# Two weight subtractions on GpSimd instead of VectorE, with a new order of the instructions

## The chip, the core and the metric

The kernel runs on one core of a Trainium2 chip. The metric is the device time in microseconds from the start to the end of one execution. The core has five engines that work side by side, each on its own list of instructions in a fixed order: PE (TensorE, the matmuls; PEld is its loading of weights), DVE (VectorE), ACT (ScalarE), POOL (GpSimd), and SP, which here only issues DMAs. They wait for each other through semaphores.

## The reference

Attention within chunks of 64 tokens is followed by a feed-forward layer with a quadratic relu. All inputs are float32.

```python
# q, k, v: 8 batches x 8 heads x 576 tokens x 64
scores = q_c @ k_c.T / sqrt(64)           # within each chunk of 64 tokens
attn = exp(scores - max); attn = attn / (sum + 1e-9)
x = (attn @ v_c)                          # as 4608 tokens x 512
h = x @ w_in                              # w_in 512 x 2048
g = where(h >= 1, h, where(h <= -1, 0, (h + 1) ** 2 / 4))
out = g @ w_out                           # w_out 2048 x 512
```

The two weights come as 64-bit floats; the kernel reads them as pairs of 32-bit words.

## The kernel before, in words

**Tiles.** The 4608 tokens are nine tiles of 512. `w_in` and `w_out` are cut into 16 blocks each (wi0 to wi15, wo0 to wo15). A product in full precision is three matmuls: each operand is kept as a high part (rounded to the matmul's format) and a low part (what the rounding left), and high x high, high x low and low x high are summed in PSUM.

**Preparing weights** (`prepare`, L433 to 479). A block lands as words; ACT scales the upper words (L444), DVE shifts (L447), ACT scales the lower words (L450), DVE adds (L455), ACT rounds to the high part (L470), and DVE subtracts to get the low part (L474). So a block costs three instructions on ACT and three on DVE.

**Stages.** First comes the attention of tile 0, in four groups of two heads: PE turns q and k (L569), ACT copies (L594), PE makes scores (L617), DVE and ACT do the softmax (L696 to L709, L702), POOL multiplies by the reciprocal sum (L714), PE turns the result back (L569), ACT copies (L725), PE multiplies by v (L638), and ACT and DVE split the result into high and low part, xh and xl (L779, L780). While PE has nothing else to do there it runs matmuls on the identity that nobody reads (L1535, called fillers here). Then the first three tiles go through the layer directly (`ffn_in` L831, the curve at L838, L841 and L842, the split at L851 and L852, `ffn_out` L866), while the blocks of weights are still being prepared and the attention of later tiles is done in between. The last six tiles go in pairs by a scheme that needs seven products of mixed blocks instead of eight (L1103). For it, sums of the weights' blocks are formed (`mix_weights`, L936 to L960), written to DRAM by POOL's DMAs (L922) and later streamed back by POOL's DMAs (L1011) into a ring of seven places; and sums of the inputs are formed for each pair (`mix_x`, L1074 to L1083). In the paired stage L1112, L1118, L1144, L1147, L1148 are the sums and the curve, and L1202 and L1203 split the middle result into high and low part.

**What sets the order.** A planner (`Plan`) takes all steps with an assumed cost for each, their inputs and outputs, plays them through in its own model of the engines and of the DMA queues, and lets each engine take the ready step with the earliest deadline. It does so twice to get deadlines and then writes the instructions in the order that results. Steps that carry an `after` (the mixing of the weights) get a deadline earlier by `EARLY`. Fillers are written wherever the model finds PE without work between two given points. So a change of one cost, or of one entry of a table, can move instructions on every engine; and how many fillers the program has is fixed when it is written.

Of the kernel before, what the change touches and what calls it, by code (L numbers as in the profile page):

```python
# [62 lines left out]
class Plan:  # L63
# [9 lines left out]
    ROUNDS = 2  # L73
    EARLY = 5.0
    PACKET = {128: 0.0128, 256: 0.0188, 512: 0.031, 1024: 0.05, 2048: 0.086, 4096: 0.22}
# [186 lines left out]
def kernel(  # L262
# [15 lines left out]
    nc = tc.nc  # L278
# [14 lines left out]
    NF = DFF // P  # L293
# [5 lines left out]
    ROWED = (0, 1)  # L299
    EARLY = 2  # L300

# [9 lines left out]
    OWN, RING5, EARLIER, LATER, SPARE = range(5)  # L311
    SCHEDULE = (
        (17, OWN), (18, EARLIER), (18, OWN), (21, EARLIER), (22, RING5), (24, RING5), (25, EARLIER), (27, OWN), (27, RING5), (33, RING5), (37, LATER), (38, OWN), (42, RING5), (43, OWN), (45, OWN), (46, OWN),
    )
# [66 lines left out]
    for w, j, names in (  # L381
# [5 lines left out]
        both = place("first", w, j, [P, 2, T], F32)  # L387
# [13 lines left out]
    plan = Plan()  # L401
# [31 lines left out]
    def prepare(w, j):  # L433
# [38 lines left out]
        def low():  # L472
            hi, lo = (weight[w, j][:, n, :] for n in range(2))
            nc.vector.tensor_tensor(  # L474
                out=placed(lo), in0=natural(yf), in1=placed(hi.bitcast(F32)), op=ALU.subtract
            )

        plan.add("act", 0.52, high, (ykey,), both)
        plan.add("dve", 0.6, low, (ykey, both[0]), (both[1],))


# [502 lines left out]
    LOADS = list(range((NTILE - MIXED) // 2 * STEPS // 2))  # L984
    for load, sooner in ((5, 1), (10, 1), (14, 1), (56, 2), (70, 1), (112, 2), (126, 1), (154, 1),):
        was = LOADS.index(load)
        LOADS.insert(was - sooner, LOADS.pop(was))
    TAKEN = {11: 1, 12: 1, 14: 1, 16: 1, 20: 1, 61: 1, 62: 1, 76: 1, 117: 1, 118: 1, 132: 1, 160: 1}
    held, SLOT, OUSTED = [(tag, -1) for tag in RING], {}, {}
# [405 lines left out]
    FIRST_SCORES, BURSTS = 4, (4, 8, 11, 15)  # L1395
    PAIRS = {0: (BURSTS[-1],), 1: (5, 12), 2: (0, 4, 9, 12)}
    HELD_BURSTS, RECALL_BURSTS, HELD_MIX_X = (0, 2, 4, 6), (6, 11), 1
    QUAD_BURSTS, OUT_BURST, MIX_X = (0, 4, 6), 1, 0
    MIX_AT = []
    for n, own in SCHEDULE:  # L1400
        m = len(MIX_AT)
        what = ("wi", m) if m < NF // 2 else ("wo", (4, 1, 5, 2, 0, 3, 6, 7)[m - NF // 2])
        MIX_AT.append((n, own, what))
# [99 lines left out]
    def mix_next(t):  # L1503
        plan.behind = 0
        mix_x(t)
        plan.behind = 0
# [68 lines left out]
```

## Time and profile before

| | |
|---|---|
| time, median of 3 runs | 797.57 us (797.56 to 798.97) |
| the profiled execution | 798.37 us, of which the span from first to last instruction 796.6 us |
| granted TensorE clock, mean | 0.999 of full speed |
| busy: PE, DVE, ACT, POOL | 99%, 86%, 63%, 22% of the span |
| chain that ended last | PE 81%, DVE 10%, DMA 3%, ACT 3%, SP's queue 2% |

The busy shares are averages over very different stages. PE counts as busy while it runs fillers too, so its 99% does not say that 99% of the span is useful work. Overlapping matmuls make each record longer than the distance between two starts; the distance is what counts.

### The profile page before, as it was taken

How to read it: one execution, taken by the hardware profiler on the slowest of the kernel's cores; microseconds unless marked ns; L12 is line 12 of the kernel's file. 1: busy time of each engine (PE TensorE's matmuls, PEld its weight loads, DVE VectorE, ACT ScalarE, POOL GpSimd, SP SyncE). 2: the span in 40 equal slices, each digit the busy share in tenths (PEclk: the TensorE clock that was granted, in tenths of full speed). 3: DMA queues.
4: the chain of work that ended last, by engine and by line, in shares of the span. 5: the costliest groups of instructions: out<-in, count | busy, mean ns of one | idle time of the engine just before them, and what ended most of it. 6: DMA issues, size and time to landing. Idle time of an engine off the chain costs nothing.

```text
span 796.6 us, 15281 instructions
## 1 busy us (share of the span) xinstructions
PE 787.3 (99%) x5660; PEld 650.2 (82%) x5660; DVE 682.8 (86%) x1089; ACT 501.7 (63%) x870; POOL 179.0 (22%) x294
## 2 busy tenths in 40 slices
PE   9999999999999999999999999999999999999997
PEld 8788888888888888888887888788878888888886
DVE  4989998798867899999969999999599986765896
ACT  5999874454555466776468646864687456636840
POOL 1100000756132233223221211111111121211211
PEclk9999999999999999999999999999999999999999
DMA  9996855979598777989899868998765697566664
GB/s 203 282 296 166 212 103 105 328 239 305 152 275 235 188 214 225 247 286 261 244 275 255 219 182 224 294 274 235 211 205 175 188 278 231 186 192 190 193 190 106
DMA packets 250571, 176.67 MB, mean 222 GB/s; under 512 B 208129, under 2 KB 216321, under 8 KB 250497
## 3 DMA queue, kind: packets, MB, share of 16 engines
q0 software_dynamic: 33344, 117.98, 46.5%
q1 hardware_dynamic: 212896, 56.66, 31.9%
q10 hardware_dynamic: 4256, 1.05, 0.7%
q8 instruction: 45, 0.74, 0.4%
q14 instruction: 30, 0.24, 0.1%
HBM read 133.17 MB, written 38.80 MB: 216 GB/s over the span
## 4 chain that ended last, share of the span: by engine, by line
PE 81%; DVE 10%; DMA 3%; ACT 3%; SPq 2%; issue 1%; DVEq 0%
PE ps_o L1103 34%; PE ps_o L866 17%; PE ps_h L831 15%; PE ps_h L1103 11%; PE ps_a L617 2%; DVE big_wo L1112 1%; DVE big_wo L1148 1%; PE ps_h L638 1%; DVE gl L1203 1%; DVE big_wo L1203 1%; DMA words_wi<-in_moe_w_in_dram 1%; DVE big_wo L1122 1%; DMA q_sb_both<-in_q_dram 1%; SPq L493 1%; DMA aT_both<-qT_both 1%
## 5 line engine op out<-in xcount | busy, mean ns | idle before, releaser
L1011 POOL DMA_DIRECT2D big_wi<-mixed x144 | 77.0, 535 | 328.2 <-PE ps_o L1103 175.6
L831 PE MATMUL ps_h<-xh,parts_wi 128*128 128x512 f32 x376 | 125.4, 393 | 0.7 <-DVE r L842 0.7
L866 PE MATMUL ps_o<-parts_wo,gh 128*128 128x512 f32 x384 | 119.8, 393 | 0.0
L1103 PE MATMUL ps_o<-big_wo,big_wi 128*128 128x512 f32 x396 | 96.5, 389 | 0.0
L1103 PE MATMUL ps_o<-gh,big_wi 128*128 128x512 f32 x264 | 88.5, 390 | 0.0
L1103 PEld LDWEIGHTS ps_o<-big_wo,big_wi 128*128 128x128 f32 x396 | 74.3, 188 | 15.5
L866 PEld LDWEIGHTS ps_o<-parts_wo,gh 128*128 128x128 f32 x384 | 71.1, 188 | 15.4 <-ACT tmp L888 0.4
L831 PEld LDWEIGHTS ps_h<-xh,parts_wi 128*128 128x128 f32 x376 | 70.6, 188 | 15.8 <-DVE r L842 1.1
L1103 PE MATMUL ps_h<-big_wi,big_wi 128*128 128x512 f32 x312 | 75.9, 390 | 0.0
L866 PE MATMUL ps_o<-parts_wo,gl 128*128 128x512 f32 x192 | 74.9, 390 | 0.0
L831 PE MATMUL ps_h<-xl,parts_wi 128*128 128x512 f32 x188 | 73.2, 389 | 0.0
L1103 PE MATMUL ps_o<-big_wi,big_wi 128*128 128x512 f32 x282 | 71.0, 392 | 1.2 <-ACT tmp L1118 1.2
L1202 ACT CAST big_wo<-big_wo 128x512 fp32r<-128x512 f32 x76 | 47.1, 621 | 35.0 <-PE ps_o L1103 20.2
L1103 PEld LDWEIGHTS ps_h<-big_wi,big_wi 128*128 128x128 f32 x312 | 58.4, 188 | 12.2
L1202 ACT CAST gh<-big_wo 128x512 fp32r<-128x512 f32 x76 | 47.1, 620 | 27.4 <-PE ps_o L1103 23.2
L1103 PEld LDWEIGHTS ps_o<-big_wi,big_wi 128*128 128x128 f32 x282 | 52.3, 188 | 14.2 <-ACT tmp L1118 2.7
L1147 ACT ACTIVATE big_wo<-big_wo 128x512 f32<-128x512 f32 x96 | 60.0, 632 | 1.6
L1103 PEld LDWEIGHTS ps_o<-gh,big_wi 128*128 128x128 f32 x264 | 49.6, 188 | 10.7 <-ACT big_xl L795 0.2
L1112 DVE TENSOR_TENSOR big_wo<-ps_o,big_wo 128x512 f32<-128x512 f32 x84 | 56.0, 680 | 1.9 <-PE ps_o L1103 1.8
L1203 DVE TENSOR_TENSOR gl<-big_wo,gh 128x512 fp32r<-128x512 f32 x76 | 51.8, 681 | 6.2 <-ACT gh L1202 6.2
L1203 DVE TENSOR_TENSOR big_wo<-big_wo,big_wo 128x512 fp32r<-128x512 f32 x76 | 51.7, 683 | 4.4 <-ACT big_wo L1202 4.3
L1103 PE MATMUL ps_o<-gl,big_wi 128*128 128x512 f32 x132 | 51.4, 389 | 0.0
(283 smaller groups left out, 1647.6 us busy)
## 6 DMA issues: line engine op xcount, KB each, us to landing
big_wi<-mixed POOLq DMA_DIRECT2D x144, 512.0 KB, 4.7
big_wo<-mixed POOLq DMA_DIRECT2D x24, 512.0 KB, 4.8
words_wi<-in_moe_w_in_dram SPq DMA_DIRECT2D x16, 512.0 KB, 6.4
words_wo<-in_moe_w_out_dram SPq DMA_DIRECT2D x16, 512.0 KB, 6.6
v_sb<-in_v_dram SPq DMA_DIRECT2D x52, 128.0 KB, 4.6
q_sb_both<-in_q_dram SPq DMA_DIRECT2D x104, 64.0 KB, 4.2
k_sb_both<-in_k_dram SPq DMA_DIRECT2D x104, 64.0 KB, 3.8
mixed<-parts_wi POOLq DMA_DIRECT2D x24, 256.0 KB, 4.6
```

Of the source, the lines that this page charges most:

```text
L493: queue.dma_start(out=dst[j * C:(j + 1) * C], in_=heads_rows(src, t, 2 * g + j).rearrange("c p d -> p c d"),)
L617: nc.tensor.matmul(out=scores[i * C:(i + 1) * C, half, n * C:(n + 1) * C], lhsT=qT[rows, at], rhs=kT[rows, at], start=True, stop=True,)
L638: nc.tensor.matmul(out=values[half][h * C:(h + 1) * C, n * C:(n + 1) * C], lhsT=v_sb[rows, of:of + C], rhs=rhs, start=True, stop=True,)
L831: nc.tensor.matmul(out=ps, lhsT=weight["wi", j][:, half, kc * P:(kc + 1) * P], rhs=x(), start=(kc == 0 and i == 0), stop=(kc == KC - 1 and ...
L866: nc.tensor.matmul(out=acc, lhsT=x[:, cols], rhs=weight["wo", j][:, half, :], start=(j == 0 and i == 0), stop=(j == NF - 1 and i == 2),)
L1011: nc.gpsimd.dma_start(out=place_of(tag).bitcast(F32), in_=mixed[n][:, rows, :])
L1103: nc.tensor.matmul(out=bank, lhsT=parts[part], rhs=rhs, start=fresh and begin and k == 0, stop=end and k == 2, skip_group_check=not fresh,)
L1112: plan.add("dve", cost, lambda: nc.vector.tensor_tensor(out=o(), in0=b, in1=x(), op=ALU.add), (bkey, xkey), (okey,), after=after)
L1122: plan.add("dve", 0.6, lambda: nc.vector.tensor_tensor(out=o(), in0=x(), in1=y(), op=ALU.subtract), (xkey, ykey), (okey,))
L1147: plan.add("act", 0.52, lambda: nc.scalar.square(out=r(), in_=r()), (), (rkey,))
L1202: plan.add("act", 0.52, lambda: nc.scalar.copy(out=h(), in_=x()), (key,), (hkey,))
L1203: plan.add("dve", 0.6, lambda: nc.vector.tensor_tensor(out=l(), in0=x(), in1=h().bitcast(F32), op=ALU.subtract), (key, hkey), (lkey,))
```

## The change

The low part (L474) of wi0 and of wo0 is computed by POOL instead of DVE, with 1.1 us as its assumed cost. `EARLY` goes from 5 to 50 us. The tables that place the mixing of the weights, the loads of the ring, the attention of a later tile and the mixing of the inputs (`SCHEDULE`, `LOADS`, `TAKEN`, `PAIRS`, `MIX_X`, the sequence of `wo`) get other entries, and `mix_x` starts with another rank. The number of DVE's instructions falls by two, POOL's rises by two; the other engines do the same work.

```diff
-    EARLY = 5.0
+    EARLY = 50.0
...
     OWN, RING5, EARLIER, LATER, SPARE = range(5)
     SCHEDULE = (
-        (17, OWN), (18, EARLIER), (18, OWN), (21, EARLIER), (22, RING5), (24, RING5), (25, EARLIER), (27, OWN), (27, RING5), (33, RING5), (37, LATER), (38, OWN), (42, RING5), (43, OWN), (45, OWN), (46, OWN),
+        (18, OWN), (19, EARLIER), (20, RING5), (21, EARLIER), (22, EARLIER), (22, OWN), (24, RING5), (27, RING5), (34, RING5), (37, LATER), (37, LATER), (37, OWN), (43, OWN), (43, OWN), (44, OWN), (47, OWN),
     )
...
             hi, lo = (weight[w, j][:, n, :] for n in range(2))
-            nc.vector.tensor_tensor(
+            (nc.gpsimd if j < 1 else nc.vector).tensor_tensor(
                 out=placed(lo), in0=natural(yf), in1=placed(hi.bitcast(F32)), op=ALU.subtract
             )
 
         plan.add("act", 0.52, high, (ykey,), both)
-        plan.add("dve", 0.6, low, (ykey, both[0]), (both[1],))
+        plan.add(*(("pool", 1.1) if j < 1 else ("dve", 0.6)), low, (ykey, both[0]), (both[1],))
...
-    for load, sooner in ((5, 1), (10, 1), (14, 1), (56, 2), (70, 1), (112, 2), (126, 1), (154, 1),):
+    for load, sooner in ((5, 1), (10, 1), (14, 1), (56, 4), (57, 4), (58, 3), (70, 1), (112, 3), (113, 3), (126, 1), (154, 1),):
...
-    TAKEN = {11: 1, 12: 1, 14: 1, 16: 1, 20: 1, 61: 1, 62: 1, 76: 1, 117: 1, 118: 1, 132: 1, 160: 1}
+    TAKEN = {11: 1, 12: 1, 14: 1, 16: 1, 20: 1, 22: 1, 62: 1, 76: 1, 115: 1, 132: 1, 160: 1}
...
-    PAIRS = {0: (BURSTS[-1],), 1: (5, 12), 2: (0, 4, 9, 12)}
+    PAIRS = {0: (BURSTS[-1],), 1: (4, 12), 2: (0, 4, 9, 12)}
...
-    QUAD_BURSTS, OUT_BURST, MIX_X = (0, 4, 6), 1, 0
+    QUAD_BURSTS, OUT_BURST, MIX_X = (0, 4, 6), 1, 3
...
-        what = ("wi", m) if m < NF // 2 else ("wo", (4, 1, 5, 2, 0, 3, 6, 7)[m - NF // 2])
+        what = ("wi", m) if m < NF // 2 else ("wo", (2, 1, 5, 6, 0, 4, 3, 7)[m - NF // 2])
...
     def mix_next(t):
-        plan.behind = 0
+        plan.behind = 60
         mix_x(t)
```


On SP, whose list is only DMA issues at this place, from the load of k of group 2 on. The places first_wi15 and first_wi14 take q and k of groups 2 and 3, the places v_sb0, v_sb1 and first_wo14 the values of groups 0 to 2. Before:

```order
L493 DMA first_wi14_97<-in_k_dram 64x8x64 x2
L493 DMA first_wi15_95<-in_q_dram 64x8x64 x2
L493 DMA first_wi14_97<-in_k_dram 64x8x64 x2
L420 DMA words_wi0_175<-in_moe_w_in_dram 128x4x256
L543 DMA v_sb0_70<-in_v_dram 128x4x64 x2
L543 DMA v_sb1_71<-in_v_dram 128x4x64 x2
L420 DMA words_wi1_225<-in_moe_w_in_dram 128x4x256
L543 DMA first_wo14_98<-in_v_dram 128x4x64 x2
L420 DMA words_wi2_259<-in_moe_w_in_dram 128x4x256
```

Now:

```order
L493 DMA first_wi14_97<-in_k_dram 64x8x64 x2
L420 DMA words_wi0_135<-in_moe_w_in_dram 128x4x256
L493 DMA first_wi15_95<-in_q_dram 64x8x64 x2
L493 DMA first_wi14_97<-in_k_dram 64x8x64 x2
L543 DMA v_sb0_70<-in_v_dram 128x4x64 x2
L420 DMA words_wi1_209<-in_moe_w_in_dram 128x4x256
L543 DMA v_sb1_71<-in_v_dram 128x4x64 x2
L543 DMA first_wo14_98<-in_v_dram 128x4x64 x2
L420 DMA words_wi2_269<-in_moe_w_in_dram 128x4x256
```

The load of wi0 stands in front of q and k of group 3, and the load of wi1 in front of the values of group 1. The load of wi2 has the same loads in front of it as before.

On ACT, ten rows before the curve of the first block is done (L838, L841). r0 is the middle result of wi0, ps_h0 its bank, xh1 from ps_o23 the high part of group 3. Before:

```order
L470 CAST parts_wi3_464<-tmp1_88 128x512
L779 CAST xh1_0_0_421<-ps_o23_89 128x2x4x64
L450 ACTIVATE words_wo0_324<-words_wo0_324 128x512
L444 ACTIVATE tmp_both_86<-words_wo1_327 128x512
L450 ACTIVATE words_wo1_327<-words_wo1_327 128x512
L470 CAST parts_wo0_489<-tmp0_87 128x4x4x32
L444 ACTIVATE tmp_both_86<-words_wi4_342 128x512
L838 ACTIVATE r0_80<-ps_h0_93 128x512
L838 ACTIVATE r1_81<-ps_h1_94 128x512
L841 ACTIVATE r0_80<-r0_80 128x512
```

Now, from the high part of group 3 on:

```order
L779 CAST xh1_0_0_411<-ps_o23_89 128x2x4x64
L444 ACTIVATE tmp0_87<-words_wo0_331 128x512
L470 CAST parts_wi3_465<-tmp1_88 128x512
L450 ACTIVATE words_wo0_331<-words_wo0_331 128x512
L444 ACTIVATE tmp_both_86<-words_wo1_341 128x512
L450 ACTIVATE words_wo1_341<-words_wo1_341 128x512
L838 ACTIVATE r0_80<-ps_h0_93 128x512
L470 CAST parts_wo0_493<-tmp0_87 128x4x4x32
L841 ACTIVATE r0_80<-r0_80 128x512
```

The high part of wo0 (L470 on parts_wo0) and the first step of wi4 (L444 on words_wi4) stood in front of the curve of r0 (L838) and now stand behind it. Further up on ACT, around the first step of wi2, before:

```order
L725 COPY first_wi13_99<-ps_o1_92 128x512
L779 CAST xh0_0_0_331<-ps_o23_89 128x2x4x64
L444 ACTIVATE tmp_both_86<-words_wi2_259 128x512
L450 ACTIVATE words_wi2_259<-words_wi2_259 128x512
L470 CAST parts_wi1_413<-tmp_both_86 128x512
L779 CAST xh1_0_0_421<-ps_a_90 128x2x4x64
```

Now:

```order
L725 COPY first_wi13_99<-ps_o1_92 128x512
L470 CAST parts_wi1_380<-tmp_both_86 128x512
L779 CAST xh0_0_0_320<-ps_o23_89 128x2x4x64
L444 ACTIVATE tmp_both_86<-words_wi2_269 128x512
L779 CAST xh1_0_0_411<-ps_a_90 128x2x4x64
L450 ACTIVATE words_wi2_269<-words_wi2_269 128x512
```

The high part of wi1 (L470 on parts_wi1) stood behind the first step of wi2 and now stands in front of it.

On PE, twelve rows from the turning back of the softmax of group 1 (kT_both) on; first_wo14 and first_wo15 hold the softmax of groups 2 and 3, and the one row on parts_wi0 and xl0 stands in the first product of the layer. Before:

```order
L569 MATMUL ps_o1_92<-ident_65,kT_both_76 128x128 x4
L638 MATMUL ps_a_90<-aT_both_77,v_sb0_70 64x64 x16
L1535 MATMUL ps_h0_93<-ident_65 128x128 x7
L569 MATMUL ps_o1_92<-ident_65,first_wo14_98 128x128 x4
L1535 MATMUL ps_h0_93<-ident_65 128x128
L638 MATMUL ps_o23_89<-aT_both_77,v_sb1_71 64x64 x16
L831 MATMUL ps_h0_93<-xh0_0_0_331,parts_wi0_306 128x512
L831 MATMUL ps_h0_93<-xl0_0_0_352,parts_wi0_306 128x512
L831 MATMUL ps_h0_93<-xh0_0_0_331,parts_wi0_306 128x512
L638 MATMUL ps_a_90<-first_wi13_99,first_wo14_98 64x64 x16
L1535 MATMUL ps_o0_91<-ident_65 128x128 x4
L569 MATMUL ps_o1_92<-ident_65,first_wo15_96 128x128 x4
```

Now:

```order
L569 MATMUL ps_o1_92<-ident_65,kT_both_76 128x128 x4
L1535 MATMUL ps_h0_93<-ident_65 128x128 x2
L831 MATMUL ps_h0_93<-xh0_0_0_320,parts_wi0_297 128x512
L831 MATMUL ps_h0_93<-xl0_0_0_328,parts_wi0_297 128x512
L831 MATMUL ps_h0_93<-xh0_0_0_320,parts_wi0_297 128x512
L1535 MATMUL ps_o0_91<-ident_65 128x128 x2
L569 MATMUL ps_o1_92<-ident_65,first_wo14_98 128x128 x4
L1535 MATMUL ps_o0_91<-ident_65 128x128
L638 MATMUL ps_o23_89<-aT_both_77,v_sb1_71 64x64 x16
L1535 MATMUL ps_o0_91<-ident_65 128x128
L638 MATMUL ps_a_90<-first_wi13_99,first_wo14_98 64x64 x16
L1535 MATMUL ps_o0_91<-ident_65 128x128 x2
```

The first product of wi0 now stands in front of the turning of group 2; behind the last row the first product of wi1 follows, and only then the turning of group 3. There are fewer fillers: over the whole program 38 where there were 42.

In the second output half of the first pair, DVE now does the mixing of the next pair's inputs (`mix_x`) earlier. The last low parts that the half's products need (L1203) therefore stand further back: the first of the four for the last product seven instructions, the others eleven to thirteen. PE has four products of the next pair (six matmuls each) more in front of the products that use the first of them, and five more in front of those that use the others. From the end of this half on the lists of DVE and ACT are the same as before, but for some twenty places in the next pair's half. The second pair's first three loads of the ring are issued three or four loads earlier.

## Rows read from the trace of the kernel before

**Rows 1.** Waits of PE over the whole span: in total, times, longest.
```profile
PE ps_h L1535 <- POOL ident masks.py:199: 1.4, 1, 1.4
PE ps_o L1103 <- ACT tmp L1118: 1.2, 3, 0.7
PE ps_h L831 <- DVE r L842: 0.7, 1, 0.7
PE ps_o L617 <- ACT first_wi L594: 0.6, 1, 0.6
```

**Rows 2.** Busy time by stretch: PE, PEld, DVE, ACT, POOL, clock, DMA.
```profile
25.00:30.00 5.00, 5.00 (x58) 4.13 (x57) 4.33 (x9) 5.00 (x10) 0.60 (x1) 1.00 1.04 392
30.00:35.00 5.00, 5.00 (x23) 3.79 (x21) 4.22 (x10) 5.00 (x11) 0.00 (x0) 1.00 1.15 291
60.00:70.00 10.00, 10.00 (x76) 8.03 (x75) 9.32 (x18) 10.00 (x20) 0.00 (x0) 1.00 0.56 118
```

**Rows 3.** Chain that ended last, 0 to 60 us: start, duration, what.
```profile
17.20 7.41 DMA words_wi<-in_moe_w_in_dram
...
24.62 0.12 ACT tmp_both L444
...
25.87 0.49 ACT parts_wi L470
...
32.29 0.55 ACT parts_wo L470
32.84 0.57 ACT tmp_both L444
33.41 0.97 ACT r L838 x2
...
34.93 0.70 DVE r L842
...
35.68 2.34 PE ps_h L831 x9
...
44.14 2.72 PE ps_h L831 x12
```

**Rows 4.** Timeline of PE at the start: start, duration, what, [idle before].
```profile
7.41 1.06 PE L1535 MATMUL ps_h<-ident 128*128 128x128 f32 x8
...
17.55 0.69 PE L617 MATMUL ps_o<-first_wi,first_wo 64*64 64x64 f32 x32 [0.56 <-ACT first_wi L594]
...
22.85 0.50 PE L831 MATMUL ps_h<-xh,parts_wi 128*128 128x512 f32 x1
...
30.77 0.39 PE L831 MATMUL ps_o<-xh,parts_wi 128*128 128x512 f32 x1
```

**Rows 5.** Timeline of SP's DMA issues at the start.
```profile
7.79 1.46 SPq L493 DMA_DIRECT2D first_wi<-in_q_dram  x2
...
10.65 0.63 SPq L420 DMA_DIRECT2D words_wi<-in_moe_w_in_dram  x1
```

**Rows 6.** Landing of w_in blocks: the first, and all issued in 0 to 45.
```profile
words_wi<-in_moe_w_in_dram SPq DMA_DIRECT2D x1, 512.0 KB, 5.7
...
DMA to landing us min/median/max: 4.8/7.4/9.6
```

**Rows 7.** Timelines of DVE and POOL at the start.
```profile
20.31 1.26 DVE L474 TENSOR_TENSOR parts_wi<-tmp,parts_wi 128x512 fp32r<-128x512 f32 x1
...
40.99 0.68 DVE L474 TENSOR_TENSOR parts_wo<-tmp,parts_wo 128x512 fp32r<-128x512 f32 x1
...
19.98 1.04 POOL L714 TENSOR_TENSOR first_wo<-first_wo,sm_both 128x512 f32<-128x512 f32 x1 [2.83 <-ACT aT_both L725]
24.29 1.31 POOL L714 TENSOR_TENSOR first_wo<-first_wo,sm_both 128x512 f32<-128x512 f32 x1 [3.26 <-DVE sm_both L709]
```

**Rows 8.** Timelines of DVE and PE in the second output half, 430 to 476.
```profile
467.89 0.69 DVE L1203 TENSOR_TENSOR gl<-big_wo,gh 128x512 fp32r<-128x512 f32 x1
...
472.39 0.39 PE L1103 MATMUL ps_o<-gl,big_wi 128*128 128x512 f32 x1
```

## The prediction

> **What bounds the kernel now.** I read the waits of PE first [rows 1], then the busy time by stretch [rows 2], then the chain that ended last [rows 3], and only then the timelines of the start. The waits are small: 1.4 us at the very beginning, 0.6 in the attention of tile 0, 0.7 before the second round of the layer's first products, and 1.2 in three places of the paired stage. From 25 us on PE is full and at full granted clock, and ACT is full too, still at 60 to 70 us [rows 2]. So the kernel is PE's work plus what comes before PE gets dense. Its real work is the same before and after; time can only come out of fillers, out of the waits, or out of new waits. The chain shows what sets the start: the load of wi2 is issued by SP at 17.20 and takes 7.41 us; at 24.62 ACT begins with it, works on without a stop, and only at 34.93 DVE frees the bank of the first block (L842), so that PE goes on at 35.68 [rows 3]. PE had been waiting for 0.7 us by then. From there the chain is mostly PE.
>
> **The change part by part.**
>
> *The two subtractions.* DVE loses two L474; 0.68 us is the undisturbed duration [rows 7], so 1.36 us of DVE. POOL gains two of a form that the trace shows only as L714, with 1.04 and 1.31 us [rows 7]. Per block the low part is then 0.36 to 0.63 us later. For wi0 it lies beside the attention of tile 0: the first product now stands ahead of the turning of group 2, but the chain through wi2 ends later than that. For wo0 it lies under nine matmuls of wi3 that stand in front of its use. At 2.72 us for 12 matmuls [rows 3] these take 2.0 us. I cost both at nothing; without the cover it would be 0.4 to 0.6 us each. DVE's gain is nothing by itself either: DVE is not what PE waits for at the start, except behind ACT.
>
> What the trace has against POOL is one row: the L474 at 20.31 took 1.26 us while POOL's L714 ran from 19.98 [rows 7], 0.58 us more than the undisturbed one. That may happen once for each new POOL instruction, 1.2 us of DVE at most, as much as the move saves there. The Trainium skill ("SBUF — State Buffer", "Who interferes with whom") says that a VectorE instruction with both inputs in SBUF and a GpSimd instruction that reads SBUF exclude each other, and that the later one waits for the whole of the other; the trace agrees with 1.26 us against 0.68. By that rule the price is 0.6 us per meeting on DVE, and the sum for PE stays the same while the chain runs over ACT.
>
> *The loads.* wi0 goes out where the first load of q of group 3 went, at 7.79 instead of 10.65 [rows 5], 2.9 us earlier. q and k of group 3 are pushed back by one issue (0.63 us) and by the block's 512 KB. The load of wi2 has the same loads in front of it, so I take 17.20 and 24.62 for it again. Ends: landings of w_in blocks took 4.8 to 9.6 us [rows 6], which for wi2 would be 2.6 us earlier or 2.2 later; 7.4 is the value of wi2 itself and the median.
>
> *ACT between wi2 and the curve of r0.* Three instructions leave this stretch: the high part of wi1 (0.49 us), which now runs while ACT waits for wi2's landing, the high part of wo0 (0.55) and the first step of wi4 (0.57), which move behind L838 [rows 3]. Between L838 and L841 there was the L838 of r1, half of 0.97 us, and there is now the high part of wo0, 0.55: 0.07 more. Together 0.49 + 0.55 + 0.57 - 0.07 = 1.54 us. ACT has no gap in this stretch [rows 2], so L842, and PE behind it, comes 1.54 us earlier: at 34.14 instead of 35.68. What is late next is PE itself. It has four fillers fewer; four cost 1.06 us [rows 4]. With the waits of 0.6 and 0.7 us gone [rows 1] PE could be there 2.4 us earlier. So ACT still ends last, and PE waits there some 0.9 us (2.4 - 1.54). The ends of this term are 0 (the old wait is refilled by something else) and -2.4.
>
> *The early stage from 36 us on.* PE arrives 1.54 us earlier, ACT is full until 70 us, and only the high part of wi1 and the xh of group 1, next to 1.0 us, have been taken out of its list by being done before 24.62. If PE used every result as soon as ACT had it, 0.5 us would be given back. But the low part of wo2 ends at 41.7 [rows 7], and its first matmuls come only after the 12 matmuls from 44.14, at 46.9 [rows 3]: 5 us of slack. I take 0, with 0 and +0.5 as ends.
>
> *Paired stage.* The three waits on L1118 (1.2 us) stand where the lists of ACT and DVE are the same; I keep them. In the second output half DVE's low part at 467.89 moves back by seven instructions, at no more than that row's 0.69 us each 4.8 us; it has been ready since 468.6 and is used at 472.39 [rows 8], a slack of 3.8. Alone that would cost 1.0 us. But PE has 24 more matmuls in front of it, 5.4 us at the pace of 2.72 us for 12. So 0; ends -1.2 (all three waits go) and +1.0.
>
> **The sum.** On the profiled execution 798.37 us: -1.54 (ACT's stretch) + 0 + 0 + 0 = 796.83. That execution is 0.80 above the median of 797.57, so the forecast for the median is 796.0.
>
> **Rivals.**
>
> *More than the start.* The wi2 load comes a little earlier and PE's own limit counts (-2.4), or the waits of the paired stage go too. For it speaks that the new tables concern mainly that stage, and that PE does mixing work earlier; against it that around those waits nothing moved. Half of both, -2.4 and -0.6: 797.57 - 3.0 = 794.6.
>
> *It does not arrive at the end.* The 1.54 us are there at 34 us and are given back: 0.5 in the stretch where ACT is full, 0.6 by a meeting of DVE and POOL, and 0.4 of the up to 1.0 at the low parts. Sum 0: 797.5. For it speaks how full ACT and DVE are; against it the slack of 5 and 3.8 us that I found in the places looked at.
>
> *Slower: wi0 lands late and ACT stands behind it.* Its first step (L444) now stands in front of the exp of group 1, and SP's load of the values of group 1 must wait until wi0 has landed, since in the program each load of SP waits for the one eight places before it. With the 5.7 us of before [rows 6] it lands at 13.5. With the worst 9.6 us it lands at 17.4. The exp would then be 3.3 us late, the issue of wi2 as much, and the sum -1.54 + 3.3 = +1.8: 799.3. It decides from a landing of about 7.5 us after the issue, where the gain is gone. For it speaks that the load's 512 KB now meet the loads of q and k that are still under way; against it that wi0 needed 5.7 us before, with as many loads under way [rows 6].
>
> *The change does nothing for the order.* That is excluded: the lists show the new places.
>
> **How the numbers follow.** What a measurement here can tell from no change is about 0.2%, 1.6 us, so the bound for faster is 795.97. Forecast 0.52, more than the start 0.16, does not arrive 0.20, slower 0.12. The forecast's own range, 795.2 to 796.8, has the bound in its middle; I give 0.26 of its 0.52 to faster and 0.26 to same. Faster: 0.26 + 0.16 = 0.42, and 0.02 from the edge of the third case, 0.44. Same 0.26 + 0.18 = 0.44, slower 0.12. The range from 794.2 to 798.5 reaches to both neighbours and leaves out half of the slow case and the tail of the second.
>
> **What would show it.** Right: L444 on wi0 ACT starts near 13.5; wi2's first step still near 24.6; L842 of r0 near 33.4 and PE's products of wi3 near 34.1, with a wait of around 0.9 us ahead of them; the waits on L1118 in the paired stage as before. Wrong in size: wi2's landing moved, or PE's wait at that place is zero. Wrong in kind: a gap of ACT behind wi0 before 17 us, or new waits of PE between 40 and 320 us or near 470 us.

## The result: 805.17 us, slower by 0.9%, and the profile after

| | before | after |
|---|---|---|
| median of 7 runs each | 797.8 us (797.56 to 798.97) | 805.17 us (801.71 to 809.01) |
| ratio, 95% interval | | 1.0093 [1.0064, 1.0123] |
| the profiled execution (its span) | 798.37 us (796.6) | 809.01 us (807.2) |

The forecast was 796.0. The time lies outside the stated range of 794.2 to 798.5, on the other side. The runs also lie further apart: 7.3 us from the fastest to the slowest, against 1.4. The profiled execution is the slowest of the seven, 3.8 us above the median. In the experiments below, one execution each of e5, e6 and e12 was disturbed (1600, 2034 and 1232 us) and is left out of every number.

PE's waits of the changed kernel, which answer to [rows 1] (total, times, longest):

```profile
PE ps_a L617 <- issue: 3.3, 1, 3.3
PE ps_h L831 <- ACT big_xl L795: 1.9, 1, 1.9
...
PE ps_h L638 <- DVE r L842: 1.2, 1, 1.2
PE ps_o L569 <- DMA first_wi<-in_q_dram: 1.0, 1, 1.0
...
PE ps_h L831 <- DVE xl L780: 0.9, 1, 0.9
```

The last two are in the start, where there is also one of 0.4 us for L842 ahead of wi3. The first three are new, in stretches where before had no wait at all. Where they stand is read from PE's timeline (start, duration, what, idle before):

```profile
271.20 0.34 PE L638 MATMUL ps_h<-aT_both,v_sb 64*64 64x64 f32 x3 [1.24 <-DVE r L842]
280.95 0.50 PE L831 MATMUL ps_h<-xh,parts_wi 128*128 128x512 f32 x1 [1.87 <-ACT big_xl L795]
...
498.14 0.65 PE L617 MATMUL ps_a<-kT_both,qT_both 64*64 64x64 f32 x32
502.12 0.58 PE L617 MATMUL ps_a<-kT_both,qT_both 64*64 64x64 f32 x24 [3.33 <-issue]
```

I call the first two place A and the last one place B. Behind each the granted clock was at its lower level (1.2 instead of 2.4 GHz) for at least 3 us. In these rows of busy time by stretch it is the third number from the end: 1.00 up to 280 us, 0.50 behind A and 0.50 behind B.

```profile
270.00:280.00 10.00, 7.88 (x152) 6.48 (x152) 9.19 (x16) 4.06 (x6) 7.38 (x11) 1.00 0.87 261
281.50:284.50 3.00, 3.00 (x8) 2.34 (x7) 3.00 (x5) 1.56 (x2) 1.25 (x2) 0.50 0.94 369
503.50:506.50 3.00, 3.00 (x9) 2.32 (x8) 2.22 (x3) 1.50 (x3) 0.53 (x1) 0.50 0.64 104
```

What the lower clock costs is read from the chain that ended last (start, duration, what): 24 products of the same form behind A and 18 us later, and six behind B and a little later.

```profile
280.95 7.31 PE ps_h L831 x24
...
299.02 5.44 PE ps_h L831 x24
...
502.70 2.26 PE ps_h L1103 x6
504.96 2.28 PE ps_o L1103 x6
507.24 1.39 PE ps_h L1103 x6
```

At A that is 7.31 - 5.44 = 1.9 us, so A costs 1.24 + 1.87 + 1.87 = 5.0 us. At B it is (2.26 - 1.39) + (2.28 - 1.39) = 1.8, so B costs 3.33 + 1.8 = 5.1 us. Together that is 10.1 of the 10.6 us by which the two profiled spans differ. It shows in the starts of the same work too: the paired stage begins 4.5 us later than in before (317.89 against 313.40), and the last wait on L1118 stands 10.2 us later (600.4 against 590.2).

The start went part of the way that was forecast. Rows of the chain of the changed kernel that answer to [rows 3]:

```profile
9.61 5.97 DMA first_wi<-in_q_dram
...
15.71 0.63 PE ps_o L569 x4
...
34.98 2.33 PE ps_h L831 x9
```

PE takes up wi3 at 34.98 instead of 35.68. By 120 us nothing of that is left: the same twelve products (L866) behind the attention matmuls begin at 120.64 in before's chain and at 120.61 in this one.

**Place A, link by link.** The first wait is for a bank that the curve (L842, on DVE) still reads. ACT had finished its part of the curve (L841) at 268.54, but DVE's list has sums of weights (L936) in front of L842, which starts only at 270.47. In before it starts at once: L841 ends at 269.56, L842 begins at 269.59. ACT, then DVE of the changed kernel:

```profile
267.91 0.63 ACT L841 ACTIVATE r<-r 128x512 f32<-128x512 f32 x1
...
267.92 1.28 DVE L936 TENSOR_TENSOR big_xl<-parts_wo 128x512 f32<-128x512 f32 x2
...
270.47 0.68 DVE L842 SCALAR_TENSOR_TENSOR r<-ps_h,r 128x512 f32<-128x512 f32 x1
```

The second wait is for a buffer. ACT's copy of an attention result into xl (L795) at 280.31 had to wait until a store of mixed weights out of the same buffer had landed. POOL issued these stores as soon as ACT had rounded their sums (0.26 us of waiting for ACT), and ACT had waited 0.60 us for the sums, which DVE made from 267.92 to 272.41. In front of them in POOL's list is a store of another mix (e), which had waited for ACT and DVE in the same way. The chain, then ACT's and POOL's timelines:

```profile
264.33 6.81 issue
...
274.81 5.40 DMA mixed<-big_xl
...
280.31 0.59 ACT big_xl L795
```

```profile
272.45 1.14 ACT L959 CAST big_xl<-big_xl 128x512 fp32r<-128x512 f32 x2 [0.60 <-DVE big_xl L936]
...
271.17 0.72 POOL L922 DMA_DIRECT2D mixed<-e  x1 [6.83 <-ACT e L959]
...
273.37 2.89 POOL L922 DMA_DIRECT2D mixed<-big_xl  x4 [0.26 <-ACT big_xl L959]
```

Two mixes go through the buffers of xl, and the second one's stores are issued at 273.37 to 276.3. In before only one does; POOL and ACT there:

```profile
263.67 1.45 POOL L922 DMA_DIRECT2D mixed<-big_xl  x2 [0.32 <-DVE big_xl L960]
```

```profile
272.22 1.07 ACT L795 COPY big_xl<-ps_h 128x512 f32<-128x512 f32 x2 [0.81 <-PE ps_h L638]
```

Its stores are issued some seven us before L795 needs the buffer, and L795 waits for PE alone.

**Place B** is a stop inside a burst of 128 small attention matmuls: some 100 of them had run, the rest had not, no semaphore is named, and both parts of L617 have the same operands. What moved in that time is in the view of the DMA queues. Between 484 and 499 us it has no packet of queue q8; between 499 and 501 us it has one (packets, MB, share):

```profile
q8 instruction: 1, 0.02, 3.2%
```

Queue q8 loads instructions, in 45 packets of 16 KB over the whole program (0.74 MB by the page of the profile); they follow PE's progress, one for each 250 or so of its 11,300 instructions. The packet falls into PE's stop: in steps of 0.1 us it begins to move between 499.5 and 499.6 us, and PE goes on at 502.12. In before the one in question (the 31st of 45 in both) moved at 483.2 us, 8 us ahead of the burst, which begins at 491.3:

```profile
q8 instruction: 1, 0.02, 5.2%
```

### The profile page after: what moved, and what is told of

The parts are those of the page before. It is cut to its first block, busy times and chain, and to the rows that moved or that the text cites. A ratio compares the mean times of both kernels' runs of the same rounds, so it can differ in the third digit from the quotient of the medians.

```text
span 807.2 us, 15251 instructions
## 1 busy us (share of the span) xinstructions
PE 790.1 (98%) x5652; PEld 650.5 (81%) x5652; DVE 685.7 (85%) x1087; ACT 502.5 (62%) x870; POOL 180.9 (22%) x296
## 4 chain that ended last, share of the span: by engine, by line
PE 81%; DVE 7%; issue 3%; ACT 3%; DMA 3%; POOL 1%; SPq 1%; ACTq 0%; DVEq 0%; POOLq 0%
PE ps_o L1103 35%; PE ps_h L831 15%; PE ps_o L866 14%; PE ps_h L1103 11%; PE ps_a L617 1%; POOL mixed L922 1%; DMA k_sb_both<-in_k_dram 1%; PE ps_h L638 1%; DVE big_wo L1148 1%; DMA first_wi<-in_q_dram 1%; ACT big_wo L1144 1%; DVE gl L1203 1%; DVE big_wo L1112 1%; DMA mixed<-big_xl 1%; DVE big_wo L1203 1%
## 5 line engine op out<-in xcount | busy, mean ns | idle before, releaser
L866 PE MATMUL ps_o<-parts_wo,gh 128*128 128x512 f32 x384 | 119.7, 393 | 0.0
L1103 PE MATMUL ps_o<-big_wo,big_wi 128*128 128x512 f32 x384 | 93.7, 390 | 0.0
L1103 PE MATMUL ps_o<-gh,big_wi 128*128 128x512 f32 x272 | 92.0, 391 | 0.3 <-ACT big_wo L1118 0.3
L1103 PEld LDWEIGHTS ps_o<-big_wo,big_wi 128*128 128x128 f32 x384 | 71.9, 188 | 15.4 <-DVE big_wo L1203 0.5
L866 PEld LDWEIGHTS ps_o<-parts_wo,gh 128*128 128x128 f32 x384 | 71.1, 188 | 15.0
L866 PE MATMUL ps_o<-parts_wo,gl 128*128 128x512 f32 x192 | 74.9, 390 | 0.0
L1103 PE MATMUL ps_o<-big_wi,big_wi 128*128 128x512 f32 x252 | 64.3, 396 | 0.9 <-ACT tmp L1118 0.9
L1203 DVE TENSOR_TENSOR gl<-big_wo,gh 128x512 fp32r<-128x512 f32 x76 | 51.7, 681 | 7.3 <-ACT gh L1202 7.3
L1103 PEld LDWEIGHTS ps_o<-big_wi,big_wi 128*128 128x128 f32 x252 | 47.7, 191 | 12.6 <-ACT tmp L1118 2.0
L1203 DVE TENSOR_TENSOR big_wo<-big_wo,big_wo 128x512 fp32r<-128x512 f32 x76 | 51.4, 681 | 4.5 <-ACT big_wo L1202 4.5
L838 ACT ACTIVATE r<-ps_h 128x512 f32<-128x512 f32 x47 | 28.1, 597 | 40.4 <-PE ps_h L831 38.5
```

The costliest lines, as they stand in the source:

```text
L838: plan.add("act", 0.48, lambda: nc.scalar.activation(out=r, in_=ps, func=AF.Relu, bias=0.5, scale=0.5), (pkey,), (rkey,))
L866: nc.tensor.matmul(out=acc, lhsT=x[:, cols], rhs=weight["wo", j][:, half, :], start=(j == 0 and i == 0), stop=(j == NF - 1 and i == 2),)
L1103: nc.tensor.matmul(out=bank, lhsT=parts[part], rhs=rhs, start=fresh and begin and k == 0, stop=end and k == 2, skip_group_check=not fresh,)
L1203: plan.add("dve", 0.6, lambda: nc.vector.tensor_tensor(out=l(), in0=x(), in1=h().bitcast(F32), op=ALU.subtract), (key, hkey), (lkey,))
```

## The experiments

### One part at a time: e1 to e4

**e1**: `(nc.gpsimd if j < 1 else nc.vector)` back to `nc.vector`, and the planner's `("pool", 1.1)` back to `("dve", 0.6)`.

> The changed kernel with the two low parts back on VectorE, everything else as changed. My theory (two places): the loss does not come from the two subtractions but from (A) the mixing of the weights near 258 to 282 us, where PE waits 1.2 and 1.9 us and then runs at half clock for 3.4 us, about 4 us together, and (B) a stop of 3.3 us in the middle of a burst of attention matmuls near 499 us, again with half clock behind it, about 5.5 us, in some executions. So this kernel stays slow: 801 to 809 us, with A at its place. Rival (GpSimd): the subtractions on GpSimd disturb VectorE or the planner; then this kernel goes back to 798 or below.

**e2**: these two edits alone, made in the kernel before.

> The kernel before with only the two low parts on GpSimd, all tables as before. Theory (two places): no stop at 258 to 282 us and none near 499 us; the start gains the 0.7 us that the changed kernel has at 35 us, so 797 us, within 1 us of before. Rival (GpSimd): slower by several us, 801 or more.

**e3**: `EARLY = 50.0` back to `5.0`.

> The changed kernel with EARLY at 5 us instead of 50, so that the mixing of the weights no longer goes in front of the curve and the attention. Theory (two places, with two mixes at once in the buffers of xl at step 37 as the cause of A): A stays, about 4 us, time 801 to 805. Rival (EARLY): the 1.2 and 1.9 us near 271 and 281 us are gone and the time falls by 4 us to 797 to 804, depending on the stop near 499 us.

**e4**: `SCHEDULE` and the sequence of the wo blocks back.

> The changed kernel with SCHEDULE and the sequence of the wo blocks as before; EARLY 50 and all else as changed. Theory (two places): A is gone (one mix in the buffers of xl at step 37), so 4 us less: 797 to 798 where the stop near 499 us does not come, up to 803 where it does. Rival (EARLY): A stays or moves elsewhere between 40 and 320 us, 801 or more even without the stop near 499 us.

| | median (range), us | ratio to before |
|---|---|---|
| e1 | 811.38 (809.07 to 813.17) | 1.0162 [1.0135, 1.0189] |
| e2 | 805.38 (803.63 to 806.91) | 1.0090 [1.0067, 1.0112] |
| e3 | 806.77 (805.51 to 812.78) | 1.0121 [1.0082, 1.0160] |
| e4 | 806.39 (803.59 to 807.75) | 1.0097 [1.0072, 1.0121] |

My theory of two places (e1 to e4 were to show that A and B alone make the loss) fell with e2: the kernel before with nothing but the two subtractions moved is as slow as the changed one, and its tables are before's. Its stops are elsewhere, at 233, 325 and 449 us. e1 kept A (a wait of 3.4 us on L795) and was slower still; e3 and e4 lost the wait on L795, got others near 285, 323 and 336 us (e3) or 240, 323 and 340 us and place B (e4), and gained nothing. So it is no single table. What all five have in common is that the planner made a new order.

The stop in e2 shows what such an order runs into. The chain of e2: DVE's copy of the layer's result (L886) into tmp must wait for the store of tmp, which took 7.56 us from issue to landing, and PE waits for the bank.

```profile
225.05 7.56 DMA out_dram<-tmp
...
232.63 0.70 DVE tmp L886
...
233.38 0.98 PE ps_o L866 x3
```

### The order or the subtractions: e5, e6, e7

**e5**: before, with both subtractions issued to GpSimd while the planner still counts them as DVE's, so that no list changes but for these two.

```diff
-            nc.vector.tensor_tensor(
+            (nc.gpsimd if j < 1 else nc.vector).tensor_tensor(
```

> The order of before kept on every engine; only the two subtractions are issued to GpSimd (the planner still counts them as VectorE's). Theory now (the new order loses the time, not the subtractions): the time of before within 0.2%, 796.5 to 799. Rival (the subtractions on GpSimd cost by themselves): 800 or more, with VectorE's rows near them lengthened and PE late at 36 us.

**e6**: the reverse: only the planner's line changed (order of e2), issued to VectorE.

> The order that the planner makes of before's tables when it counts the two subtractions as GpSimd's, but with both issued to VectorE. Theory (order): slow like the same order with GpSimd, 803 to 808, with waits of PE between 220 and 340 us. Rival (subtractions on GpSimd): back at 798.

**e7**: the kernel plans twice, with before's tables and both subtractions issued to GpSimd. It takes the order of e2 for what the planner starts in its first 45 us (`UNTIL = 45.0`) and before's order for the rest:

```diff
+    upto = next(at for at, (start, _, _) in enumerate(new) if start > UNTIL)
+    done = {n for _, n, _ in new[:upto]} - {None}
+    rest = [x for x in old if x[1] not in done and (x[1] is not None or x[0] > UNTIL)]
+    for _, _, step in new[:upto] + rest:
+        step()
```

> Both orders joined: the new one (before's tables, subtractions on GpSimd) for what the planner starts in its first 45 us, and before's order for all the rest. Theory (order): PE takes up wi3 near 33.9 us as in the new order instead of 35.7, the later stretch has no stop between 220 and 340 us, time 796 to 797.5. Rival (an earlier start alone shifts the later stages against their transfers and costs the time): 800 or more, with waits of PE between 220 and 340 us though the order there is before's.

| | median (range), us | ratio |
|---|---|---|
| e5 | 797.66 (797.26 to 800.37) | 1.0000 [0.9989, 1.0010] |
| e6 | 803.27 (798.93 to 807.56) | 1.0056 [1.0034, 1.0078] |
| e7 | 798.81 (796.80 to 804.17) | 1.0020 [1.0001, 1.0038] |

In before's order the subtractions on GpSimd cost nothing that can be measured. The new order of before's tables costs 0.6% with VectorE subtracting (e6) and 0.9% with GpSimd (e2). Whether the 0.3% between them is a price of GpSimd in that order is open, since the intervals overlap. The changed kernel's own order with VectorE subtracting was not run: e1 has another order, since the planner counted the subtractions as DVE's there. With before's order behind 45 us most of the loss is gone. What e7 still loses stands in its profile at place B:

```profile
490.76 0.69 PE L617 MATMUL ps_a<-kT_both,qT_both 64*64 64x64 f32 x33
493.75 0.57 PE L617 MATMUL ps_a<-kT_both,qT_both 64*64 64x64 f32 x23 [2.31 <-issue]
```

The order of the work there is before's, which has no such stop. But there are four fillers fewer ahead of it: 16 instructions of PE, since one filler is two weight loads and two matmuls in the trace.

### PE's instructions: e8 to e11, e15

**e8**: each filler of the changed kernel as two of 64 columns.

> The changed kernel with every filler (a matmul on the identity of 128 columns) as two of 64 columns: same work, same order, but some 150 instructions more on PE's list, all before 30 us. Theory (the stop near 499 us is a fetch of PE's instructions that starts too late; the fetch falls elsewhere when the list is shifted, about 17 us earlier against the burst): no stop of 3 us near 499 us, the stop near 281 us stays, times 801 to 804 and none of 807 to 809. Rival (the stop is bound to that burst and its data): the 3 us at 499 us stay in the profile and the times spread from 801 to 809 as before.

**e9**: the changed kernel with four fillers more at 20 us.

> The changed kernel with four more fillers where PE waits 0.86 us for the low part of the first input (21 us), so that PE's list has as many instructions as before's (16 more) from there on. Theory (the stop near 499 us is PE's instruction fetch, and where the fetches fall against the burst decides): start within 0.3 us of the changed kernel's, no fetch that begins 10 us late near 490 us, no stop near 499 us; the waits near 271 and 281 us stay; times 800 to 804. Rival (the stop belongs to the burst and its transfers): stop and late fetch stay, 801 to 809.

**e10**: before with four fillers fewer.

```diff
-        return lambda: nc.tensor.matmul(
+        return lambda: [made.append(0)] + [nc.tensor.matmul(
             out=bank[:, :P], lhsT=ident, rhs=ident, start=True, stop=True
-        )
+        ) for _ in range(0 if len(made) in (25, 29, 31, 34) else 1)]
```

> The kernel before, order and subtractions as they were, with four fillers fewer at 16 to 22 us, so that PE's list is as long as the changed kernel's from there on (16 instructions fewer). Theory (instruction fetch): the fetch that began at 483.2 us now begins late, near 491 us, and PE stops for 1 to 3 us in the burst near 494 us; times 798 to 804, with a wider spread than before. Rival (the order of the work decides): 797.2 to 799 as before, no stop.

**e11** and **e15**: e7 with four fillers more, at 20 us, and spread over two waits.

> The joined order (new until 45 us, before's after it) with four more fillers at 20 us, so that PE's list is as long as before's. Theory (instruction fetch): PE takes up wi3 near 33.7 us, no late fetch near 482 us, no stop near 494 us; time 796.0 to 797.0 with the narrow spread of before, about 1.5 us faster than before. Rival (the earlier start disturbs the later stages): stop near 494 us stays, 798 to 804.

> The joined order (new until 45 us, before's after it) with four more fillers, one at 12 us and three at 20 us, where PE waits anyway. Theory (the start's gain is real but small, 0.7 us, and the list is as long as before's, so no late fetch): PE at wi3 near 33.7 us, no stop in the burst near 493 us, median 797.0 to 797.8, 0.5 us below before. Rival (the start is given back by 320 us): 797.8 to 798.5, the same as before.

| | median (range), us | ratio | place B in the profile |
|---|---|---|---|
| e8 | 816.09 (811.85 to 820.94) | 1.0236 [1.0183, 1.0289] | none at 499; "issue" 1.36 us in the burst at 338 |
| e9 | 805.39 (804.00 to 806.46) | 1.0093 [1.0075, 1.0110] | none |
| e10 | 799.45 (798.33 to 805.05) | 1.0031 [1.0010, 1.0052] | 1.09 us at 494 |
| e11 | 798.13 (796.74 to 799.82) | 0.9999 [0.9989, 1.0010] | none |
| e15 | 797.76 (796.55 to 799.82) | 0.9995 [0.9986, 1.0005] | none |

e10 is the clean test: before's order to the last instruction, four useless matmuls fewer, and place B is there. The burst begins at 491.23. Its second part, and q8 between 491 and 493 us (none moved from 484 to 491):

```profile
492.33 0.65 PE L617 MATMUL ps_a<-kT_both,qT_both 64*64 64x64 f32 x32
494.06 0.58 PE L617 MATMUL ps_a<-kT_both,qT_both 64*64 64x64 f32 x24 [1.09 <-issue]
```

```profile
q8 instruction: 1, 0.02, 2.9%
```

Three of its ten runs are above 803.5 us; of 19 of before beside it none is above 800.3. And e7 with the four fillers put back (e11, e15) has no stop. So 16 instructions decide when the packet moves. With them it moved at 483 us, 8 us before the burst; without them it moved only within the burst (at 491.4 us in e10 and in e7).

The other profiles bear this out. In this burst six of the nine with 38 fillers have a stop of 0.2 us or more with no semaphore (the changed kernel, e3, e4, e6, e7, e10), and none of the ten with 42. In all six PE goes on 2.3 to 2.7 us after the packet began to move: 491.4 and 494.06 in e10, 491.4 and 493.75 in e7, 499.5 and 502.12 in the changed kernel, 497.3 and 499.73 in e4. In e13, which has the changed kernel's list, PE waited 0.8 us for DVE just ahead of the burst (at 499.43); the packet moved at 496.5, and there is no stop. So the stop is as long as the packet is late. That PE's sequencer had run up to the burst's wait and could not ask earlier fits the times, but no view shows it.

e9 shows the limit of this: B is gone and the runs lie closer together, but the median stays. In its profile the second wait of A is there (2.0 us on L795), and a wait of 0.75 us near 407 us that the changed kernel's profiled run did not have; the wait at 271 us is not there. Its span is 5.6 us above before's: 1.96 for L795, 1.9 for the lower clock behind it (22 products in 6.92 us instead of 5.0 at the pace of 2.72 for 12), 0.75, and 0.4 at 368 us make 5.0 of it. So, as far as four runs tell, B makes the spread of the changed kernel and not its median. e8 bought its shift with 9 us at the start (PE at wi3 at 44.41), so its time says nothing on B; its profile does, as the stop moved to another burst.

### What makes place A: e12 to e14

**e12**: `(37, LATER), (37, LATER), (37, OWN)` becomes `(37, LATER), (37, OWN), (37, OWN)`.

> The changed kernel with one of the two mixes that step 37 puts into the buffers of xl (LATER) put into its own buffers instead (OWN). Theory (A comes from the stores of the second mix out of xl, which the split of the attention, L795, must wait for): the 1.9 us before the products at 281 us are gone, and so the half clock behind them, 2 to 4 us less in runs that have no stop near 499 us: 798 to 806. Rival (A comes from the stage's load of VectorE and of transfers, wherever the mixing writes): a wait of 1 us or more remains between 260 and 300 us, 801 to 809.

**e13** and **e14**: after and before with half of the rows of q and k loaded from tile 2 on (`out=dst[r:r + Q, :4]`, `in_=rows[:4]`).

> The changed kernel, same order on every engine, but from the attention of tile 2 on the loads of q and k bring only half of the rows (the rest keeps old values), so SP's queue and the DMA engines have some 100,000 packets of 128 bytes fewer. Theory (landings): the stops come where an engine's list stands behind a transfer that lands later than the order assumes; with the transfers relieved, the 1.2 and 1.9 us near 271 and 281 us and the half clock behind them are gone, and the time is 796 to 799. Rival (VectorE's and ScalarE's lists themselves are in the wrong order): the waits stay within half of their size, 801 to 808.

> The control: the kernel before with the same half loads of q and k. Theory (landings): before has hardly a wait that a transfer ends, so it gains at most 1 us: 796.5 to 798.5, and the distance to the changed kernel with half loads shrinks from 7 us to 2 or less. Rival (order alone): the distance stays 5 us or more.

e12: 805.53 us (three runs), 1.0095 [1.0073, 1.0117]. The wait at 281 us is gone, which fits that the second mix in xl made it; but e12 is a new order too. Some of the mixing moved back (the stores of e are issued at 283.33 and 288.85 us instead of 271.17 and 276.52), and PE waits elsewhere, at 325 us:

```profile
PE ps_o L638 <- DVE tmp L886: 3.2, 1, 3.2
```

In e13 and e14 the other half of q and k keeps old values; 57,000 of the 250,600 DMA packets are gone (I had expected 100,000). e13: 805.98 us, 1.0089 [1.0068, 1.0111]; e14: 797.5, 0.9989 [0.9980, 0.9998]. The distance between the two is 8.5 us, and the wait on L795 in e13 is even larger:

```profile
PE ps_h L831 <- ACT big_xl L795: 2.3, 1, 2.3
```

My theory of late landings fell. The store at A is not late because SP's queue is full of q and k: with half of them it took 6.0 us to land in e13, against 5.4 in the changed kernel. It is issued late, with the lists of DVE, ACT and POOL in front of it. The wait at 271 us is not in e13's profile, nor in e9's, though their lists are the changed kernel's (e9 has four fillers more); so that link of A is not there in every execution.

### A new order without the edit: e16 to e18

**e16**: before, with nothing but the planner's cost of the low part at 0.63 instead of 0.6.

> The kernel before with nothing changed but the planner's assumed cost of the low part, 0.63 us instead of 0.6; both subtractions on VectorE, same tables, as many fillers. The planner makes another order from the second half of the first tiles on. Theory (any newly planned order meets landings that before's does not): slower, 800 to 808, with stops between 160 and 340 us at other places than in the changed kernel. Rival (the change's own tables or the move to GpSimd cost the time): 797.5 to 799.

**e17** and **e18**: this order and before's joined at 300 us, one way and the other.

> Two orders joined, both with the subtractions on VectorE and before's tables: the one planned with 0.63 us for the low part (802.1 us by itself) for all that the planner starts before 300 us, and before's order for the rest. Theory (the stretch at the beginning of the paired stage, 320 to 345 us, where that order waits 0.7 and 1.2 us, holds most of its loss of 4 us): 798 to 799.5, no waits at 320 to 345 us. Rival (the loss is laid down before 300 us and only shows later): 801 to 803, the waits stay.

> The other way round: before's order until 300 us, and the order planned with 0.63 us for the rest. Theory (the stretch from 320 to 345 us holds the loss): 800 to 802.5, with the waits of 0.7 and 1.2 us near 322 and 328 us. Rival (laid down before 300 us): 797.5 to 799, like before.

| | median (range), us | ratio |
|---|---|---|
| e16 | 802.13 (801.54 to 802.36) | 1.0045 [1.0030, 1.0059] |
| e17 | 799.34 (798.49 to 801.75) | 1.0014 [1.0005, 1.0024] |
| e18 | 803.38 (803.02 to 803.87) | 1.0064 [1.0048, 1.0081] |

A mere 0.03 us in an assumed cost loses 4 us. Both halves of that order lose, but most of it is behind 300 us. e18 loses more than e16 itself; its profile has a wait of 1.6 us just behind the place where the two orders are joined, which e16's has not, so that much of its loss may come from the joint. PE in e18 there and as the paired stage begins:

```profile
303.81 0.50 PE L831 MATMUL ps_h<-xh,parts_wi 128*128 128x512 f32 x1 [1.63 <-DVE r L842]
...
324.39 1.66 PE L1103 MATMUL ps_o<-big_wi,big_wi 128*128 128x512 f32 x6 [0.68 <-ACT big_wo L1118]
325.99 0.27 PE L638 MATMUL ps_o<-aT_both,v_sb 64*64 64x64 f32 x2
...
328.72 1.65 PE L1103 MATMUL ps_o<-big_wi,big_wi 128*128 128x512 f32 x6 [0.64 <-ACT tmp L1118]
```

The first wait, 0.68 us, comes from PE's own list: six products that need a bank which ACT is still emptying (L1118) stand directly behind the twelve before them, and the attention matmuls only behind these six. In before the attention matmuls stand in between:

```profile
318.84 2.88 PE L1103 MATMUL ps_o<-big_wi,big_wi 128*128 128x512 f32 x12
321.65 0.27 PE L638 MATMUL ps_o<-aT_both,v_sb 64*64 64x64 f32 x2
```

The second wait has this chain:

```profile
324.86 3.15 DMA out_dram<-tmp
...
328.08 0.59 ACT tmp L1118
```

L888 copies the last result of the layer's direct part into tmp; L1118 needs tmp next and must wait until the store, which took 3.15 us, has landed. In before L888 stands seven us earlier on ACT, at 316.86, and PE has no wait until 427 us:

```profile
316.86 0.59 ACT L888 COPY tmp<-ps_o 128x512 f32<-128x512 f32 x1
...
324.15 0.58 ACT L1118 COPY tmp<-ps_o 128x512 f32<-128x512 f32 x1
```

The first of the two waits, 0.7 us at 320 to 328 us, is in the profiles of e1, e2, e3, e4, e6, e12, e16 and e18, and in none with before's order at that place (e5, e7, e10, e11, e14, e15, e17). The changed kernel does not have it either: there the attention matmuls begin at 326.15, directly behind the twelve products. So e16 to e18 show what a new order can cost, and not what this one cost.

## Why the prediction was wrong

**The step that failed** is in the sum: it has no term for the whole new order beyond the places where before waited. I looked at those places and at two low parts, found slack or unchanged lists, and put everything else at nothing without a reason; "around those waits nothing moved" says nothing of places where before had no wait. The terms that I did work out for the paired stage held: the waits on L1118 come to 1.2 us in both kernels (0.9 and 0.3 in the changed one), and there is no wait near 470 us. What the runs showed in place of the zero is a new order that makes new waits. In the profiled execution they are at 271 and 281 us in the stretch of the mixing (5.0 us with the lower clock) and in the burst at 499 us (5.1 us). New waits of PE between 40 and 320 us were the prediction's own sign of being wrong in kind. That the order costs and not the subtractions is shown for before's tables (e5 against e6); the fillers that the order leaves out, which I counted only as a gain of 1.06 us, brought the stop in the burst (e10).

**The two subtractions** at nothing: right in before's order (e5, 1.0000).

**Contention of POOL and DVE**: there, once for the two new POOL instructions, and its price was right in kind. While POOL's L474 ran from 19.18 us, DVE's L708 took 1.07 us; the next one took 0.17:

```profile
19.42 1.07 DVE L708 TENSOR_SCALAR sm_both<-sm_both 128x8 f32<-128x8 f32 x1
...
24.30 0.17 DVE L708 TENSOR_SCALAR sm_both<-sm_both 128x8 f32<-128x8 f32 x1
```

That is 0.9 us where I had 0.6. L708 has one input, and the rule that I had quoted is for two. The Trainium skill ("SBUF — State Buffer", "Who interferes with whom") says that a `tensor_scalar` too can use the ports that VectorE shares with GpSimd, if its operands allow it, and that the one that comes first keeps them for its whole instruction while the other waits. The trace agrees: POOL's instruction ended at 20.46 and L708 at 20.49. I had said that it does not reach PE. It did: xl (L780) came 0.9 us late and PE waited 0.86 us for it.

**The loads**: ACT began with wi0 at 13.56, as forecast (13.5), and with wi2 at 24.85 (24.62), though SP issued that load at 18.35 and not at 17.20. The price fell on q of group 3, which I named as pushed back and did not cost: PE waited 1.0 us for it at 15.71. (In e9 and e13 this wait is below 0.2 us.)

**ACT's stretch**, -1.54 us: it came to -0.70. Not ACT's list but PE's own products ended last ahead of the curve (L838); behind it L838, the high part of wo0, L841 and L842 take their time, and PE waits 0.41 us for them, not 0.9:

```profile
31.85 0.69 PE ps_h L831 x3
...
32.57 0.60 ACT r L838
```

The 0.7 us are also less than the spread of this place: with before's order PE came there at 35.68 in one execution and at 34.36 in another (e5), and with the changed kernel's at 34.98 and at 33.88 (e13).

**From 36 us on**: I took 0 and kept +0.5 as an end. All of the gain was given back by 120 us, as in the rival "does not arrive at the end"; which of that rival's items did it, if any, is not shown. e15, which has the start of e2's order and before's order behind it, is level with before.

**The rivals**: the slow one (wi0 lands late) did not happen; the slower side came from a mechanism that I did not have. A change that makes a planner search anew should have had more than 0.12 on the slow side: before's order has 1.2 us of waits after 36 us, so a new one had little to gain there and much to lose. One sum is wrong as well: "more than the start" says "half of both" and takes the 2.4 us whole; half of both would be 1.8 us, and so 795.8.

**Open**: why the stops of one and the same order differ from run to run (e6: 798.9 to 807.6; the waits at 271 us and near 407 us), and which entry of the tables keeps the attention matmuls in front of the six products near 322 us in the changed kernel, where before's tables lose that place when planned anew. No version with all of its loads was clearly faster than before; e15 comes closest.

## What to carry to other kernels

Where a planner or a search writes the order, a small edit is a new order, and its price can have little to do with the edit: keep the order fixed and swap only the instruction (e5), and plan anew without the edit (e16), before any cause is looked for in the edit. In a profile with hardly any waits, do not ask only what moves around the waits that are there, but which buffers are freed by a transfer, and how far ahead of the next use the transfer is issued. And count the instructions ahead of a burst of small matmuls: removing idle work can move a fetch into it.

## What the hardware showed that I had not expected

- Four fillers fewer, 16 instructions, put a stop of 1 to 3.3 us into a burst 470 us later. A packet of the instruction queue moves within that burst, and PE goes on 2.3 to 2.7 us after it began to move (e10, e7, the changed kernel; gone in e11 and e15).
- A matmul on the identity took no less time with half the columns: behind the first stretch, 16 of 64 columns took 1.90 us in e8 and 8 of 128 columns 1.06 us in the changed kernel. So fillers cost by their number:

```profile
17.31 1.90 PE L1535 MATMUL ps_h<-ident 128*128 128x64 f32 x16
```

```profile
9.90 1.06 PE L1535 MATMUL ps_h<-ident 128*128 128x128 f32 x8
```

- After a wait of 1.9 us (A) or 3.3 us (B) the granted clock stood at half for at least 3 us, which cost 1.9 and 1.8 us more. But the length of the wait alone does not tell: behind the 2.31 us of e7 (494 to 499 us) and a wait of 3.06 us in e3 (336 to 341 us) the granted clock stayed at 1.00.
